# Fused attention and gated MLP on one core: weight loads moved in among the activations, and the start's hand-written order replaced

## The chip, the cores and the metric

The kernel runs on one core of a Trainium2 chip. Its engines work side by side, each through its own queue in order: TensorE (PE, matrix products), VectorE (DVE), ScalarE (ACT), GpSimd (POOL) and SyncE (SP), which here issues every DMA. The metric is the device time of one execution in microseconds (us); lower is better.

## The reference, cut to what matters

```python
def mab(q, kv):                      # attention without projections
    s = scale * (q @ kv.transpose(0, 2, 1))
    a = softmax(s)                   # over the last axis
    return a @ kv
h   = mab(I, x)                      # 32 inducing rows attend to 12416 rows of x, for each of 4 batches
y   = mab(x, h)                      # every row of x attends to the 32 rows of h
g   = y @ w_gate                     # 128 -> 1536
out = (g * sigmoid(g) * (y @ w_val)) @ w_out     # 1536 -> 128
```

x is float32. The three weight matrices arrive as float64, so they are 8 bytes an element in memory.

## The kernel before

**The main loop.** For each of four batches the rows of x are cut into 25 column blocks of 512 or 480 rows, and each block into 12 tiles (the 12 groups of 128 of the 1536 hidden units). A tile is a *front* (two PE products into PSUM, gate and value, from the block's attention weights `stack` and the projected weights `tw`), a *gate* (SiLU on ACT), a *value* (a product on DVE), a split of the result into a high and a low part (`h_hi`, mostly by ACT, and `h_lo`, mostly by POOL), and a *back* (three PE products with `wo_lo`, `wo_hi`, `wo_hi` into the output). The fronts run some tiles ahead of the backs. Steps of the next batch's attention are put in between.

**The start.** Everything up to the first tiles of batch 0 is a list of tokens, `START` and then `SECOND`, run one after the other; that order is the order of each engine's queue. For batch 0 x comes in seven chunks of 14 blocks of 128 rows (the last has 13). `lx` loads a chunk with features on the partitions, `ln` loads it with rows on the partitions; a chunk for which `ln` is left out is turned by PE transposes and copied out of PSUM (by ACT or DVE). `s1` scores a chunk and evacuates it on DVE, `ma`/`mb` find the maximum of a group of chunks, `e1` is the exponential on ACT, `eT` turns it in 32 by 32 blocks on DVE, `hq` accumulates h on PE. Chunks 0 to GA-1 form one group with its own maximum, the others a second. `ha`, `hb`, `hc`, `hd` put the groups together and give hT and hTs (h turned; the second one scaled). Steps `z0` to `z8` make the first block's attention weights by a short path of its own, and `pa`, `pk`, `pb`, `pm`, `pc` project one sixth of the gate and value weights with hT.

**The weights.** Nine pieces of 512 KB each (J0 to J5 of gate and value, o0 to o2 of the output) are loaded with `ld` and turned from float64 to float32 on the chip (class `Piece`): `X` and `low` on ACT, then `sh` and `jn` on DVE, then `add` on POOL. The output pieces are also split, `hi` on ACT and `lo` on POOL.

**Block 0** of batch 0 is an exception (`u.whole`): its backs use the joined float32 output weights as one product each, without a split of h, and the split output weights are made ready by the end of that block.

Of the kernel before, what the change touches and what calls it, by code (L numbers as in the profile page):

```python
# [76 lines left out]
jn:J3 pa:2 f:2 g:1 add:o0 m:0 pk:2 X:J4 sum:1 f:3 pm:2 add:J3 rec:1 m:1 g:2 X:o1 k:0 pa:3 pc:2 g:3 low:J4 sh:J4 m:2 f:4 f:5 jn:J4 k:1 pk:3 sh:o1 g:4
m:3 no:1:1 pm:3 k:2 at:1 X:J5 sh:J5 pc:3 g:5 low:J5 jn:J5 low:o1 jn:o1 add:J4 pa:4 add:J5 f:6 m:4 pk:4 m:5 g:6 pb:4 k:3 f:7 pa:5 m:6 add:o1 ah:1:1 f:8
al:1:0 g:7 X:o2 pk:5 sh:o2 g:8 low:o2 k:4 pm:5 f:9 jn:o2 pc:5 k:5 f:10 sp:1 m:7 k:6 m:8 f:11 g:9 add:o2 m:9 g:10 g:11 m:10 m:11 hi:o0 lo:o0 hi:o1
lo:o1  # L80
# [31 lines left out]
def induced_set_attention_then_swiglu(ctx: ExitStack, tc: tile.TileContext, xt, xn, ind, wgv, wo, out):  # L112
# [58 lines left out]
    class Piece:  # L171


        def __init__(self, work, k, i):
# [11 lines left out]
        def X(self):
            nc.scalar.activation(out=self.t.bitcast(F32), in_=self.hw.bitcast(F32), func=AF.Copy, scale=2.0 ** -112)

        def sh(self):
            nc.vector.tensor_scalar(out=self.t, in0=self.t, scalar1=3, scalar2=0x7FFFFFF8, op0=ALU.logical_shift_left, op1=ALU.bitwise_and)  # L190

        def jn(self):
            nc.vector.scalar_tensor_tensor(out=self.t, in0=self.hw, scalar=0x80000000, in1=self.t, op0=ALU.bitwise_and, op1=ALU.bitwise_or)
# [675 lines left out]
```

## Time and profile before

| what | value |
|---|---|
| device time, three executions | 1376.99, 1377.46, 1377.83 us |
| their median | 1377.46 us |
| profiled execution, first to last instruction (its span) | 1374.8 us |
| busy in the span: PE, ACT, DVE, POOL | 99%, 91%, 87%, 86% |
| granted clock of PE | 1.00 all through |

The profiled execution's own time is its span, 1374.8 us; the median of the timed executions is 2.7 us above it, and that difference is taken as the part outside the span. A time in a row counts from the start of the span. "Busy" is the share of time in which an engine has an instruction in flight; instructions of one engine overlap, so the distance from start to start says more about an engine's pace than the length of one row.

### The profile page before, as it was taken

How to read it: one execution, taken by the hardware profiler on the slowest of the kernel's cores; microseconds unless marked ns; L12 is line 12 of the kernel's file. 1: busy time of each engine (PE TensorE's matmuls, PEld its weight loads, DVE VectorE, ACT ScalarE, POOL GpSimd, SP SyncE). 2: the span in 40 equal slices, each digit the busy share in tenths (PEclk: the TensorE clock that was granted, in tenths of full speed). 3: DMA queues.
4: the chain of work that ended last, by engine and by line, in shares of the span. 5: the costliest groups of instructions: out<-in, count | busy, mean ns of one | idle time of the engine just before them, and what ended most of it. 6: DMA issues, size and time to landing. Idle time of an engine off the chain costs nothing.

```text
span 1374.8 us, 25215 instructions
## 1 busy us (share of the span) xinstructions
PE 1366.1 (99%) x7459; PEld 1183.8 (86%) x7459; DVE 1195.4 (87%) x2088; ACT 1245.7 (91%) x2380; POOL 1179.8 (86%) x994
## 2 busy tenths in 40 slices
...
GB/s 370 81 96 133 160 104 114 119 56 71 38 130 160 94 143 112 67 62 37 44 72 119 192 80 95 123 73 52 44 38 45 39 47 39 39 46 38 43 44 22
DMA packets 50680, 119.49 MB, mean 87 GB/s; under 512 B 11376, under 2 KB 28272, under 8 KB 50544
## 3 DMA queue, kind: packets, MB, share of 16 engines
...
## 4 chain that ended last, share of the span: by engine, by line
PE 97%; ACT 1%; DMA 1%; DVE 1%; issue 0%; SPq 0%; DVEq 0%
PE o L737 18%; PE gv L694 18%; PE gv L695 18%; PE o L738 18%; PE o L739 18%; PE gv L275 2%; PE o L323 1%; PE o L275 1%; DMA xt_sb<-xt 1%; PE o L734 0%; ACT silu L700 0%; PE gv L424 0%; PE gv L267 0%; ACT xn_sb L184 0%; DVE eT L313 0%
## 5 line engine op out<-in xcount | busy, mean ns | idle before, releaser
L718 POOL TENSOR_TENSOR h_lo<-h,h_hi 128x512 fp32r<-128x512 f32 (+1 forms) x889 | 1088.6, 1250 | 147.7 <-ACT h_hi L716 104.7
L700 ACT ACTIVATE silu<-gv 128x512 f32<-128x512 f32 (+1 forms) x1200 | 704.8, 589 | 95.5 <-PE gv L694 69.9
L708 DVE TENSOR_TENSOR h<-gv,silu 128x512 f32<-128x512 f32 (+1 forms) x891 | 590.9, 669 | 90.5 <-PE o L738 50.7
L716 ACT CAST h_hi<-h 128x512 fp32r<-128x512 f32 (+1 forms) x778 | 468.9, 603 | 0.8 <-DVE h L708 0.8
L694 PE MATMUL gv<-stack,tw 128*128 128x512 f32 (+1 forms) x1200 | 452.7, 377 | 1.3 <-DVE stack L544 1.0
L695 PE MATMUL gv<-stack,tw 128*128 128x512 f32 (+1 forms) x1200 | 448.2, 374 | 0.0
L737 PE MATMUL o<-h_hi,wo_lo 128*128 128x512 f32 (+1 forms) x1188 | 445.6, 375 | 0.0
L739 PE MATMUL o<-h_lo,wo_hi 128*128 128x512 f32 (+1 forms) x1188 | 443.2, 373 | 0.0
L738 PE MATMUL o<-h_hi,wo_hi 128*128 128x512 f32 (+1 forms) x1188 | 443.2, 373 | 0.0
L708 DVE TENSOR_TENSOR gv<-gv,silu 128x512 f32<-128x512 f32 (+1 forms) x297 | 201.5, 678 | 66.0 <-PE o L738 46.0
L694 PEld LDWEIGHTS gv<-stack,tw 128*128 128x128 f32 x1200 | 227.0, 189 | 33.9 <-ACT tw L416 3.0
L737 PEld LDWEIGHTS o<-h_hi,wo_lo 128*128 128x128 f32 x1188 | 224.8, 189 | 33.4 <-issue 10.6
L695 PEld LDWEIGHTS gv<-stack,tw 128*128 128x128 f32 x1200 | 227.0, 189 | 28.0 <-ACT silu L700 1.6
L739 PEld LDWEIGHTS o<-h_lo,wo_hi 128*128 128x128 f32 x1188 | 224.8, 189 | 24.3 <-POOL h_lo L718 0.3
L738 PEld LDWEIGHTS o<-h_hi,wo_hi 128*128 128x128 f32 x1188 | 224.8, 189 | 23.2
L718 DVE TENSOR_TENSOR h_lo<-gv,h_hi 128x512 fp32r<-128x512 f32 (+1 forms) x297 | 197.6, 665 | 0.8
L716 ACT CAST h_hi<-gv 128x512 fp32r<-128x512 f32 (+1 forms) x295 | 168.8, 572 | 10.1 <-DVE gv L708 8.4
L211 DVE TENSOR_REDUCE h_hi<-h 128x512 fp32r<-128x512 f32 (+1 forms) x113 | 73.7, 661 | 0.0
L748 DVE COPY ob<-o 128x512 f32<-128x512 f32 (+1 forms) x99 | 65.8, 665 | 0.2 <-PE o L739 0.2
L484 POOL TENSOR_TENSOR a_lo<-aT,a_hi 128x480 fp32r<-128x480 f32 (+2 forms) x26 | 29.9, 1151 | 0.0
L196 POOL TENSOR_TENSOR wgv_sb<-s_all 128x512 int32<-128x512 int32 x2 | 2.9, 1487 | 28.4 <-ACT s_all L184 28.4
L471 POOL TENSOR_TENSOR s_all<-s_all,sm 128x512 f32<-128x512 f32 (+2 forms) x27 | 26.1, 966 | 0.0
...
## 6 DMA issues: line engine op xcount, KB each, us to landing
...
```

Of the source, the lines that this page charges most:

```text
L211: nc.vector.tensor_reduce(out=out, in_=in_.unsqueeze(2), op=ALU.max, axis=AX.X)
L275: nc.tensor.matmul(out=ps[32 * j:32 * j + 32, 32 * (lo - b0):32 * (hi - b0)], lhsT=lhsT, rhs=st.xt[q][:, lo - CH0[q]:hi - CH0[q], j, :], s ...
L694: nc.tensor.matmul(out=u.g[:, :n], lhsT=st.w[:, wcol(0, t)], rhs=rhs, start=True, stop=True)
L695: nc.tensor.matmul(out=u.v[:, :n], lhsT=st.w[:, wcol(1, t)], rhs=rhs, start=True, stop=True)
L700: nc.scalar.activation(out=u.s[:, :u.n], in_=u.g[:, :u.n], func=AF.Silu)
L708: nc.vector.tensor_mul(out=u.h[:, :n], in0=u.v[:, :n], in1=u.s[:, :n])
L716: u.cast(out=u.hi[:, :n], in_=u.h[:, :n])
L718: eng.tensor_sub(out=u.lo[:, :n], in0=u.h[:, :n], in1=u.hi[:, :n].bitcast(F32))
L737: nc.tensor.matmul(out=o[:, :n], lhsT=wo_lo[:, ws], rhs=hi, start=(t == 0), stop=False)
L738: nc.tensor.matmul(out=o[:, :n], lhsT=wo_hi[:, ws], rhs=hi, start=False, stop=False)
L739: nc.tensor.matmul(out=o[:, :n], lhsT=wo_hi[:, ws], rhs=lo, start=False, stop=(t == NT - 1))
L748: (nc.scalar.copy if u.last else nc.vector.tensor_copy)(out=ob[:, :n], in_=o[:, :n])
```

## The change

It touches the start and the first block alone.

- **Loads.** One output piece is loaded between chunks 2 and 3 of x, and J4, o1 and J0 ahead of the only chunk that still comes by `ln` (chunk 5). Six chunks are turned on PE in place of four and a third. The chunks come in the order 0, 1, 4, 2, 3, 6, 5, and `GA` is 5: chunks 0 to 4 form the first group.
- **Buffers.** `Piece` converts in place: `X`, `sh` and `jn` of a J piece work in its final place in `wgv_sb`. The raw J pieces lie in two `tw` buffers; the projected weights later take the first of them over.
- **Finer tokens.** Steps that were one token are split into their PE part and the part of the other engine (`s1p`/`s1e`, `tp`/`te`, `mbp`/`mbe`, `hdp`/`hds`/`hdt`, `fg`/`fv`), and both lists of tokens are written anew.
- **Block 0** loses its exception: its h is split like any other (`c` on ACT, once on DVE, and `l` on POOL or DVE) and its backs are three products with the split output weights.
- **z0** scores four column groups with hTs as the stationary operand, and a DVE transpose (`z0t`) puts the result in order.

```diff
-GA = 4
+GA = 5
 START = """
-lx:0:0:4 lx:0:4:14 lx:1 lx:2 lx:3 lx:4 lx:5 lx:6 ln:4 ln:5 ln:6:0:8 ld:J0:s0 ld:J1:s1 ld:J2:t0 ld:J3:t1 wm:9
+lx:0:0:4 lx:0:4:14 lx:1 wm:9 tp:0:0 wm:6 te:0:0:1 lx:4 tp:0:3 tp:0:1 tp:0:2 te:0:1:1 s1p:0 te:0:2:0 te:0:3:1 lx:2 s1p:1 s1e:0 tp:1:0 s1e:1 tp:1:2 te:1:0:1 tp:1:3 te:1:2:0
...
 class Piece:
...
-            self.t = work[:, 2 * WP:3 * WP].bitcast(U32)
             self.w = work[:, 2 * WP:3 * WP] if k == "o" else wgv_sb[:, self.cs]
+            self.t = self.w.bitcast(U32)
...
         def z0():
             st.zps = psum()
-            for t in range(FC[0]):
-                nc.tensor.matmul(out=st.zps[:, M * t:M * t + M], lhsT=st.xt[0][:, t].rearrange("c j r -> c (j r)"), rhs=st.hTs, start=True, stop=True)
+            scores(st.hTs, 0, FC[0], st.zps)
+
+        def z0t():
+            st.z = sgl.tile([P, FC[0], M], F32, name="z")
+            nc.vector.transpose(out=st.z.rearrange("p t m -> p (t m)"), in_=st.zps[:, :M * FC[0]])
...
-        tw = att.tile([P, 2 * DFF], F32, name="tw")
-        bufs |= {f"t{i}": tw[:, 3 * WP * i:3 * WP * i + 3 * WP] for i in range(2)}
+        tws = [att.tile([P, 2 * DFF], F32, name="tw") for _ in range(2)]
+        bufs = {f"{k}{i}": t[:, 2 * WP * i:2 * WP * i + 2 * WP] for k, t in zip("tu", tws) for i in range(3)}
+        bufs |= {f"s{i}": s_all[:, 3 * WP * i:3 * WP * i + 3 * WP] for i in range(2)}
...
     def value(u):
         n = u.n
-        if u.whole:
-            u.h = hip.tile([P, WF], F32, name="h_hi")
-        else:
-            u.h = u.v if u.t in DVE_TILES else hp.tile([P, WF], F32, name="h")
+        u.h = u.v if u.t in DVE_TILES else hp.tile([P, WF], F32, name="h")
...
-        if u.whole:
-            k = t % (WP // P)
-            nc.tensor.matmul(out=o[:, :n], lhsT=pieces[f"o{t // (WP // P)}"].w[:, P * k:P * k + P], rhs=u.h[:, :n], start=(t == 0), stop=(t == NT - 1))
-        else:
-            hi, lo = turns(u.hi[:, :n]), turns(u.lo[:, :n])
-            nc.tensor.matmul(out=o[:, :n], lhsT=wo_lo[:, ws], rhs=hi, start=(t == 0), stop=False)
...
+        hi, lo = turns(u.hi[:, :n]), turns(u.lo[:, :n])
+        nc.tensor.matmul(out=o[:, :n], lhsT=wo_lo[:, ws], rhs=hi, start=(t == 0), stop=False)
+        nc.tensor.matmul(out=o[:, :n], lhsT=wo_hi[:, ws], rhs=hi, start=False, stop=False)
+        nc.tensor.matmul(out=o[:, :n], lhsT=wo_hi[:, ws], rhs=lo, start=False, stop=(t == NT - 1))
```

Three places show how the queues change. The first is the queue of SP (the loads) from the third x transfer on, before; `xn` rows are `ln` loads, `wgv` and `wo` are pieces J and o.

```order
L243 DMA xt_sb<-xt 128x1792 x3
L243 DMA xt_134<-xt 128x1792
L243 DMA xt_136<-xt 128x1792
L243 DMA xt_138<-xt 128x1664
L258 DMA xn_140<-xn 128x1792
L258 DMA xn_142<-xn 128x1792
L258 DMA xn_144<-xn 128x1024
L181 DMA s_all<-wgv 128x1024 x2
L181 DMA tw<-wgv 128x1024 x2
L181 DMA xn_sb<-wo 128x1024
L181 DMA xn_sb<-wgv 128x1024 x2
L181 DMA s_all<-wo 128x1024 x2
```

The same stretch of SP's queue after the change:

```order
L250 DMA xt_155<-xt 128x1792
L250 DMA xt_sb<-xt 128x1792
L181 DMA s_all<-wo 128x1024
L250 DMA xt_sb<-xt 128x1792
L250 DMA xt_248<-xt 128x1024
L250 DMA xt_248<-xt 128x640
L250 DMA xt_276<-xt 128x1792
L181 DMA tw<-wgv 128x1024
L181 DMA s_all<-wo 128x1024
L181 DMA tw<-wgv 128x1024
L265 DMA xn_363<-xn 128x1792
L181 DMA tw<-wgv 128x1024 x4
```

The first output piece (s_all<-wo) now stands ahead of chunk 3 of x, two J pieces and the second output piece stand ahead of the one `xn` load that is left, and four J pieces follow it.

The second place is DVE's queue around hTs, the first step behind h, before. L190 and L193 are `sh` and `jn` of a weight piece, L511 and L515 are `z1` and `z2`, L445 turns the scores of the second block.

```order
L390 TENSOR_SCALAR hTs<-gv 128x32
L190 TENSOR_SCALAR s_all<-s_all 128x512
L193 SCALAR_TENSOR_TENSOR s_all<-s_all 128x512
L190 TENSOR_SCALAR s_all<-s_all 128x512
L193 SCALAR_TENSOR_TENSOR s_all<-s_all 128x512
L511 TENSOR_REDUCE zm<-gv 128x4
L515 TENSOR_TENSOR z<-gv,zm 128x128
L445 STREAM_TRANSPOSE s_all<-gv 128x512
L207 TENSOR_REDUCE pairs<-z 128x4
```

After the change, from three rows ahead of hTs on (L196 and L199 are now `sh` and `jn`, L416 is `hc`, L551 is `z0t`, L555 and L558 are `z1` and `z2`):

```order
L199 SCALAR_TENSOR_TENSOR wgv_sb<-tw,wgv_sb 128x512
L416 SCALAR_TENSOR_TENSOR hn<-o,fac,hn 128x128
L196 TENSOR_SCALAR wgv_sb<-wgv_sb 128x512
L424 TENSOR_SCALAR hTs<-gv 128x32
L199 SCALAR_TENSOR_TENSOR wgv_sb<-tw,wgv_sb 128x512
L551 STREAM_TRANSPOSE z<-gv 128x128
L196 TENSOR_SCALAR wgv_sb<-wgv_sb 128x512
L555 TENSOR_REDUCE zm<-z 128x4
L196 TENSOR_SCALAR wgv_sb<-wgv_sb 128x512
L558 TENSOR_TENSOR z<-z,zm 128x128
L486 STREAM_TRANSPOSE s_all<-gv 128x512
L196 TENSOR_SCALAR wgv_sb<-wgv_sb 128x512
```

A `sh` now stands between `hc` and hTs, and a weight step before nearly every step of the z path.

The third place is PE's queue around the first back of block 0, before (L694 and L695 are a front, L402 and L413 `pa` and `pm`, L734 a back):

```order
L695 MATMUL gv<-stack,tw 128x512
L413 MATMUL gv<-tw,below 128x512
L734 MATMUL o<-h_hi,xn_sb 128x512
L402 MATMUL gv<-wgv_sb,hT 128x512
L694 MATMUL gv<-stack,tw 128x512
L695 MATMUL gv<-stack,tw 128x512
L694 MATMUL gv<-stack,tw 128x512
L695 MATMUL gv<-stack,tw 128x512
L734 MATMUL o<-h_hi,xn_sb 128x512
L413 MATMUL gv<-tw,below 128x512
L734 MATMUL o<-h_hi,xn_sb 128x512
```

After the change (L738 and L743 are the two halves of a front, L454 is `pm`, L787 to L789 a back):

```order
L738 MATMUL gv<-stack,tw 128x512
L454 MATMUL gv<-tw,below 128x512
L743 MATMUL gv<-stack,tw 128x512
L787 MATMUL o<-h_hi,wo_lo 128x512
L788 MATMUL o<-h_hi,wo_hi 128x512
L789 MATMUL o<-h_lo,wo_hi 128x512
L738 MATMUL gv<-stack,tw 128x512
L787 MATMUL o<-h_hi,wo_lo 128x512
L788 MATMUL o<-h_hi,wo_hi 128x512
L789 MATMUL o<-h_lo,wo_hi 128x512
L743 MATMUL gv<-stack,tw 128x512
L738 MATMUL gv<-stack,tw 128x512
```

The first back comes after five and a half fronts in place of four fronts, and it is three products instead of one. From the first back of block 1 on (12 backs and 19 fronts issued, in both kernels) the rows of PE are the same in both.

## Rows read from the trace of the kernel before

**Rows 1.** The page: its span, then busy time and share of each engine.

```profile
span 1374.8 us, 25215 instructions
...
PE 1366.1 (99%) x7459; PEld 1183.8 (86%) x7459; DVE 1195.4 (87%) x2088; ACT 1245.7 (91%) x2380; POOL 1179.8 (86%) x994
```

**Rows 2.** Busy time by stretch: PE, PEld, DVE, ACT, POOL; then PE clock, DMA share, GB/s.

```profile
12.80:19.00 6.20, 6.17 (x62) 3.68 (x66) 4.08 (x12) 3.86 (x9) 0.00 (x0) 1.00 1.03 422
38.00:50.00 12.00, 11.11 (x32) 5.12 (x30) 10.76 (x21) 11.85 (x23) 7.81 (x6) 1.00 0.00 1
...
62.06:1374.80 1312.74, 1309.18 (x6975) 1148.34 (x6973) 1150.37 (x1984) 1202.24 (x2296) 1159.02 (x967) 1.00 0.25 80
```

**Rows 3.** The chain that ended last: start, length, what; first 100 us.

```profile
3.08 9.60 DMA xt_sb<-xt
...
50.61 0.86 PE o L734 x2
```

**Rows 4.** Timeline of PE: start, length, line, tiles, count, and what idle time ended on.

```profile
36.80 0.48 PE L694 MATMUL gv<-stack,tw 128*128 128x512 f32 x1 [1.02 <-DVE stack L544]
...
62.06 0.38 PE L737 MATMUL o<-h_hi,wo_lo 128*128 128x512 f32 x1
...
63.14 0.38 PE L737 MATMUL o<-h_hi,wo_lo 128*128 128x512 f32 x1
```

**Rows 5.** Timeline of ACT, 15 to 40 us, same columns.

```profile
15.43 0.67 ACT L307 ACTIVATE s_all<-s_all,negmax 128x448 f32<-128x448 f32 x1
...
18.57 0.68 ACT L307 ACTIVATE s_all<-s_all,negmax 128x448 f32<-128x448 f32 x1
...
19.23 0.66 ACT L307 ACTIVATE s_all<-s_all,negmax 128x448 f32<-128x448 f32 x1
...
29.57 0.70 ACT L184 ACTIVATE s_all<-s_all 128x512 int32<-128x512 uint32 x1
30.16 0.70 ACT L187 ACTIVATE tw<-tw 128x512 f32<-128x512 f32 x1
...
36.69 1.28 ACT L548 ACT_TABLE_LOAD   x1
...
38.09 0.58 ACT L700 ACTIVATE silu<-gv 128x512 f32<-128x512 f32 x1
```

**Rows 6.** Timeline of DVE, 23 to 34 us.

```profile
23.60 1.65 DVE L313 STREAM_TRANSPOSE eT<-s_all 128x448 f32<-128x448 f32 x3
...
26.37 0.16 DVE L361 TENSOR_REDUCE r<-gv 128x1 f32<-128x2 f32 x1 [0.89 <-PE gv L359]
...
27.68 0.35 DVE L384 SCALAR_TENSOR_TENSOR hn<-o,fac,hn 128x128 f32<-128x128 f32 x1
...
28.72 0.42 DVE L190 TENSOR_SCALAR s_all<-s_all 128x512 uint32<-128x512 uint32 x1
29.17 0.69 DVE L193 SCALAR_TENSOR_TENSOR s_all<-s_all 128x512 uint32<-128x512 uint32 x1
29.78 0.42 DVE L190 TENSOR_SCALAR s_all<-s_all 128x512 uint32<-128x512 uint32 x1
...
30.84 0.28 DVE L511 TENSOR_REDUCE zm<-gv 128x4 f32<-128x128 f32 x1
...
33.42 0.41 DVE L190 TENSOR_SCALAR tw<-tw 128x512 uint32<-128x512 uint32 x1
33.76 0.68 DVE L457 TENSOR_TENSOR s_all<-s_all,mx2a 128x512 f32<-128x512 f32 x1
```

**Rows 7.** Timeline of POOL, 38 to 42 us.

```profile
38.31 1.52 POOL L196 TENSOR_TENSOR xn_sb<-xn_sb 128x512 int32<-128x512 int32 x1 [1.85 <-ACT sl L548]
39.79 1.29 POOL L196 TENSOR_TENSOR wgv_sb<-tw 128x512 int32<-128x512 int32 x1
41.05 1.26 POOL L471 TENSOR_TENSOR s_all<-s_all,sm 128x512 f32<-128x512 f32 x1
```

**Rows 8.** Timeline of DVE: the join that starts beside POOL's third row above.

```profile
42.07 0.79 DVE L193 SCALAR_TENSOR_TENSOR xn_sb<-xn_sb 128x512 uint32<-128x512 uint32 x1
```

More of the change, by code (lines that the diff above doesn't have):

```diff
@@ L77 @@
[L77 to L80, printed above, removed]
+sh:J1 hdp X:J3 wm:2 add:J0 hds low:J3 jn:J1 z0 sM:4:20 X:J2 z0t sh:J3 hdt lo:o0 z1 low:J2 sh:J2 pa:4 z2 X:J5 sT:4:20 pa:0 add:J1
@@ L81 @@
+fg:11 k:6 m:10 c:9:0 fv:11 g:11 l:8 l:9 m:11
 """
@@ L83 @@
     12: "sp:2",
-    13: "hi:o2",
-    14: "lo:o2",
     15: "sp:3",
@@ L186, in X, with low @@
[L186 to L193, printed above, removed]
+        def low(self, e=0):
+            if e:
+                nc.gpsimd.tensor_scalar(out=self.lw.bitcast(I32), in0=self.lw, scalar1=2.0 ** -29, scalar2=None, op0=ALU.mult)
+            else:
+                nc.scalar.activation(out=self.lw.bitcast(I32), in_=self.lw, func=AF.Copy, scale=2.0 ** -29)
@@ L366, in hacc2 @@
         def hacc2(q):
[L367 to L371 removed]
+            g = int(q >= GA)
+            n0 = (0, CH0[GA])[g]
+            if g not in st.h2:
+                st.h2[g] = ps_o.tile([P, 512], F32, name="o")
+                n = (CH0[GA], NTB - CH0[GA])[g]
+                for k in range(NG):
+                    st.hleft[g, k] = [(n - k + NG - 1) // NG, True]
             for i in range(CH[q]):
[L373 to L374 removed]
+                k = (CH0[q] + i - n0) % NG
+                left = st.hleft[g, k]
+                left[0] -= 1
                 nc.tensor.matmul(
[L376 to L377 removed]
+                    out=st.h2[g][32 * k:32 * k + 32, 0:C], lhsT=st.eT[q][:, 32 * i:32 * i + 32], rhs=st.xn[q][:, i, :],
+                    start=left[1], stop=left[0] == 0)
+                left[1] = False
         def h2_b():
@@ L666, in induced_set_attention_then_swiglu @@
             at=f["aT"], ah=lambda q, e=0: f["a_hi"](q, (same, nc.scalar.copy)[e]),
-            al=lambda q, e=1: f["a_lo"](q, dve_pool[e]), sp=f["spread"], **{f"z{i}": f[f"z{i}"] for i in range(9)})
+            al=lambda q, e=1: f["a_lo"](q, dve_pool[e]), sp=f["spread"], z0t=f["z0t"], **{f"z{i}": f[f"z{i}"] for i in range(9)})
         for token in START.split():
@@ L756, in first, with cast @@
     def first(t):
-        made.append(front(cur, 0, 0, t))
+        made.append(front_g(cur, 0, 0, t))
         pend.append(made[t])
-    short |= dict(f=first, g=lambda t: gate(made[t]), m=lambda t: value(made[t]), k=lambda t: back(pend.pop(0)))
+    def cast(t, e):
+        made[t].cast = (nc.scalar.copy, same)[e]
+        high(made[t])
+    short |= dict(fg=first, fv=lambda t: front_v(made[t]), g=lambda t: gate(made[t]), m=lambda t: value(made[t]),
+                  c=cast, l=lambda t: low(made[t]), k=lambda t: back(pend.pop(0)))
     for token in SECOND.split():
         run(token)
+    wait += [u for u in made if u.lo is None]
     cur.steps = [(slot, lambda token=token: run(token)) for slot, tokens in FIRST.items() for token in tokens.split()]
```

191 lines of the change are left out of this document (110 added, 81 removed).

## The prediction

> **What bounds the kernel now.** I read the page first: of a span of 1374.8 us PE is busy for 1366.1 [rows 1]. A busy PE need not be at its peak, so I split the span at one row. At 62.06 us PE starts the first back of block 1 [rows 4]; behind it PE is busy for 1309.2 of 1312.7 us at full clock, more than ACT, DVE and POOL [rows 2], and the change leaves the rows of every queue behind that point as they were, but for a few positions. So the part behind 62.06 us keeps its length, about 1312.7 us, and the whole effect of the change is how much earlier or later that one row starts. I call it the handover. The median of the timed runs is 2.66 us above the span; I add the shift to the median.
>
> Ahead of the handover three engines share the binding. Up to about 13 us the chain is the DMA: chunk 3 of x lands at 3.08 + 9.60 = 12.7 us [rows 3], and the loads run at 422 GB/s [rows 2]. The first exponential starts at 15.43 [rows 5], 2.75 us behind that landing. Then come h and the z path, through DVE, to the first front at 36.80, which waited for DVE's last step of `stack` [rows 4]. From 38 to 50 us ACT is busy for 11.85 of 12 us and PE for 11.11 [rows 2]: ACT leads.
>
> **The loads.** Before, four chunks of x (3.67 MB) land ahead of the first maximum. Now chunk 4 and piece o0 stand ahead of chunk 3 as well: 0.92 + 0.52 = 1.44 MB more, 3.4 us at 0.42 MB a us. Chunk 3 lands at 16.1, and with the same 2.75 us behind it the first exponential starts at 18.9. That is a loss of 3.4 us at the head. What it buys is that weight pieces come among the chunks, so o0, o1, J4 and J0 are converted while ACT would have been idle; the ACT row at 15.43 is one of seven exponentials that before were spread with gaps over 9 us.
>
> **DVE from 18.9 us to the first front.** DVE is the queue through which the path runs, and its new order puts 7 `sh` and 7 `jn` into this stretch, where the old order had three `jn` and four `sh` ahead of the first front. Start-to-start distances, from [rows 6]: three `eT` in 1.65, so 0.55 each; `sh` 0.45 when its `jn` follows (28.72 to 29.17) and 0.34 when something else follows (33.42 to 33.76), so 0.40; `jn` 0.61 (29.17 to 29.78); r, hn and its second half as one block from 26.37 to 28.03, 1.66; `z1` to `z5` with the transposed scores and their maximum as one block from 30.84 to 33.42, 2.58. The sum: seven `eT` 3.85; seven `sh` 2.8; seven `jn` 4.3; the two blocks 4.24; three copies of turned chunks and two score evacuations 2.2 (my estimate, the size of an `eT` or less); waiting for PE to score chunks 6 and 5, 0.7 (estimate); hTs, `z0t` and six one-column steps 1.6 (estimate); `pb` and the two last steps of `stack` 1.6 (estimate, at most a `jn` each). Together 21.3 us, so the first front starts at 40.2 in place of 36.80: **3.4 us later**.
>
> ACT in the same stretch is nearly as full: seven exponentials at 0.66 (18.57 to 19.23), 15 `X` and `low` at 0.59 (29.57 to 30.16), the table load and what goes with it 1.4 (36.69 to 38.09), all from [rows 5], and some 13 shorter steps of 0.1 to 0.5, 5.3 by estimate: 4.6 + 8.9 + 1.4 + 5.3 = 20.2, so its first SiLU could start at 39.1 to 39.6. It is not the later of the two, but it gives the lower end: if DVE's sum is too high, the first front cannot come before about 39.
>
> **PE from the first front to the handover.** Here the change saves. Before: 19 fronts at 0.43 us (two fifths of a tile, of which five products take 63.14 - 62.06 = 1.08 us [rows 4]) are 8.2; 12 float32 backs at 0.86 [rows 3] are 10.3; four `pa`, the same shape, 3.4; four `pm` 0.9; sum 22.8. The trace has 62.06 - 36.80 = 25.26, so PE waited 2.45. After: the fronts 8.2; 12 backs of three products, 36 x 0.216 = 7.8; three `pa` 2.6 (the fourth now stands ahead of the first front); one `pm` 0.2; sum 18.75, **4.05 less**. The price of the split backs is ten casts more on ACT and twelve `l`, nine of them on POOL at about 1.27 [rows 7]. Their cover is that nearly all of `X` and `low` is done by then. ACT in block 0 then has two operations a tile, at 0.5 each (an estimate: a SiLU lasts 0.58 [rows 5] and the next operation starts a little ahead of its end), 1.0 against PE's 1.08; without the cover it would bind.
>
> The waits in this stretch stay about the same, I take 2.5 us. The first back still stands behind the fourth and fifth front, which need PSUM buffers that `pk` and `pb` of late pieces hold, so PE waits 1.3 to 2 us there; and the stack of block 1 is sent by SP after `al`, in a block that now takes 17 us rather than 24, so its last transfer may keep the first front of block 1 for about 0.5.
>
> **The sum.** First front +3.4, products -4.05, waits +0.05: the handover moves from 62.06 to 61.45, -0.6 us, and the median from 1377.46 to **1376.9 us**. A measurement of this kernel tells about 0.2%, 2.75 us, from no change; this lies well within it.
>
> [...] One POOL `add` takes 1.52 us where its like takes 1.29 [rows 7], and a `jn` that starts at 42.07, when POOL's row at 41.05 runs until 42.31, takes 0.79 [rows 8] where one beside an idle POOL takes 0.69 [rows 6]. So the rows show some 0.1 to 0.25 us for a meeting. [...] Ten POOL operations now lie between 28 and 43 us beside as many `sh` and `jn`. [...] I take 0.5 of such cost as already inside the `jn` distances, and keep the rest as a rival.
>
> **Rivals.**
>
> (A) The helpers do not hold PE up: DVE's sum is 1 us too high (more pairs at 0.34, no waiting for chunk 5), and behind the first front PE waits only for the stack, 0.5. Then the handover is at 39.2 + 18.75 + 0.5 = 58.4, and the time 1373.8 us. For it: ACT's own sum allows 39.1, and casts are at 0.5. Against: ACT, DVE and POOL are all nearly full from 27 to 45 us, and any of them late makes the others wait. It counts as faster from a handover ahead of 59.3 on.
>
> (B) DVE and POOL block each other, at one place: between 28 and 43 us, in the joins. A `jn` or `sh` that comes while a POOL operation runs waits for its end, as the one at 42.07 may have: half of 1.29 on average, 0.64. At six meetings of ten on the path it is +3.8, the handover is at 65.3 and the time 1380.7. It counts as slower from 5.3 meetings on (3.35 / 0.64). For it: 1.52 and 0.79 above. [...]
>
> [...]
>
> **How the numbers follow.** Forecast with (C), within 0.2% of before: 0.56. (A), faster by over 0.2%: 0.25. (B), slower by over 0.2%: 0.19. The range reaches from (A)'s time, a little below, to (B)'s, a little short of it: 1373.6 to 1380.2. The forecast's own range is 1375.2 to 1378.6, from DVE's sum less 1 us with the same waits up to three meetings of 0.64.
>
> **What would show it.** Right: the first exponential near 18.9, the first front near 40, the handover within 60 to 63, and the same 1312 to 1313 us behind it. DVE nearly full from 19 to 40 us. Wrong: a first front ahead of 39 (then DVE's sum is the wrong step), one behind 42 with `jn` rows of 1 us and more (then B), a handover less than 20 or more than 23 us behind the first front (then the waits are), or a part behind the handover that differs by over 1 us, which would mean that the order of the start reaches further than I think.

## The result, and the profile after

The changed kernel takes 1386.35 us (median of five, 1385.73 to 1386.90) where the kernel before, run beside it, takes 1377.46: a ratio of 1.0064, 95% interval 1.0052 to 1.0076. It is **8.9 us slower**. The prediction was 1376.9 us, within 1373.6 to 1380.2, so it is wrong, and with it the case that it held likeliest (no change).

The page of the changed kernel, its span and its busy times, against [rows 1]:

```profile
span 1384.1 us, 25302 instructions
...
PE 1368.6 (99%) x7487; PEld 1188.8 (86%) x7487; DVE 1206.7 (87%) x2094; ACT 1253.8 (91%) x2396; POOL 1192.6 (86%) x1003
```

PE's work is hardly changed (1368.6 for 1366.1 us); the span grew by 9.3. As in the prediction I split the span at the handover, the first back of block 1. Busy time by stretch (PE, PEld, DVE, ACT, POOL, then PE's granted clock, DMA share, GB/s), against [rows 2]:

```profile
43.00:45.00 2.00, 0.00 (x0) 0.00 (x0) 1.94 (x5) 1.29 (x3) 2.00 (x2) 1.00 0.00 0
...
46.00:49.00 3.00, 3.00 (x7) 1.65 (x6) 2.89 (x5) 2.29 (x5) 1.51 (x2) 0.50 0.00 0
...
61.00:63.00 2.00, 0.00 (x0) 0.02 (x1) 1.94 (x4) 1.47 (x3) 1.27 (x1) 0.92 0.46 113
63.00:66.00 3.00, 2.99 (x7) 2.44 (x8) 1.61 (x3) 1.72 (x4) 1.01 (x1) 0.50 0.39 96
...
70.85:1384.10 1313.25, 1309.56 (x6975) 1147.07 (x6973) 1150.82 (x1984) 1202.60 (x2296) 1159.76 (x966) 1.00 0.25 80
```

The last row shows that the part behind the handover is what it was: 1313.25 us for 1312.74. So 8.8 of the 9.3 us lie ahead of it. The other rows show two stretches in which PE did nothing (43 to 45 and 61 to 63), and behind each some 3 us at a granted clock of 0.50; before, the clock stood at 1.00 there. PE's timeline gives the places (start, length, line, tiles, count, and what the idle time in brackets ended on), against [rows 4]:

```profile
45.03 0.48 PE L738 MATMUL gv<-stack,tw 128*128 128x512 f32 x1 [2.45 <-DVE stack L586]
...
63.01 0.76 PE L738 MATMUL gv<-stack,tw 128*128 128x512 f32 x1 [2.19 <-DMA stack<-a_lo]
...
63.99 0.63 PE L787 MATMUL o<-h_hi,wo_lo 128*128 128x512 f32 x1
...
70.85 0.38 PE L787 MATMUL o<-h_hi,wo_lo 128*128 128x512 f32 x1
```

The first front starts at 45.03 (36.80 before, 40.2 predicted) and waited for DVE's last step of `stack`. The first front of block 1 at 63.01 waited 2.19 us for a DMA, the stack of block 1. The row at 63.99 lasts 0.63 where the same product lasts 0.38 at the full clock. The handover is at 70.85 (62.06 before, 61.45 predicted).

Further ahead, the first exponential on ACT's timeline, and two lines of the chain that ended at 75 us (start, length, what): chunk 3's transfer, and that of the stack.

```profile
19.46 0.67 ACT L325 ACTIVATE s_all<-s_all,negmax 128x448 f32<-128x448 f32 x1
```

```profile
4.35 12.35 DMA xt_sb<-xt
...
60.90 1.97 DMA stack<-a_lo
```

Chunk 3 landed at 4.35 + 12.35 = 16.7 and the first exponential started at 19.46; the head is close to what was predicted (16.1 and 18.9). Against before, 4.0 of the 8.8 us are lost up to the first exponential (15.43 before), 4.2 from there to the first front (25.57 us for 21.37), and 0.6 from there to the handover (25.82 for 25.26). The first loss was forecast, as 3.4; in the other two stretches the forecast had 21.3 and 21.25. DVE's timeline says why its stretch took 25.57 (L392 is the last small step of h's scaling, L196 `sh`, L199 `jn`, L525 `al`):

```profile
29.32 1.15 DVE L392 TENSOR_SCALAR fac<-fac,r 128x2 f32<-128x2 f32 x1
...
30.98 1.51 DVE L199 SCALAR_TENSOR_TENSOR wgv_sb<-tw,wgv_sb 128x512 uint32<-128x512 uint32 x1
...
32.67 1.47 DVE L196 TENSOR_SCALAR wgv_sb<-wgv_sb 128x512 uint32<-128x512 uint32 x1
...
34.17 1.66 DVE L199 SCALAR_TENSOR_TENSOR wgv_sb<-tw,wgv_sb 128x512 uint32<-128x512 uint32 x1
...
36.48 1.31 DVE L196 TENSOR_SCALAR wgv_sb<-wgv_sb 128x512 uint32<-128x512 uint32 x1
...
40.22 2.16 DVE L199 SCALAR_TENSOR_TENSOR wgv_sb<-tw,wgv_sb 128x512 uint32<-128x512 uint32 x2
...
44.89 0.68 DVE L213 TENSOR_REDUCE pairs<-s_all 128x16 f32<-128x512 f32 x1
...
57.35 0.69 DVE L757 TENSOR_TENSOR h<-gv,silu 128x512 f32<-128x512 f32 x1
57.96 1.72 DVE L525 TENSOR_TENSOR a_lo<-aT,a_hi 128x512 fp32r<-128x512 f32 x1
```

And POOL's at the same times (L202 `add`, L208 `lo`, L498 `sb`, L767 `l`):

```profile
29.14 1.30 POOL L202 TENSOR_TENSOR wgv_sb<-wgv_sb,tw 128x512 int32<-128x512 int32 x1
30.56 1.38 POOL L208 TENSOR_TENSOR wo_lo<-s_all,wo_hi 128x512 fp32r<-128x512 f32 x1
...
32.56 1.29 POOL L202 TENSOR_TENSOR wgv_sb<-wgv_sb,tw 128x512 int32<-128x512 int32 x1 [0.56 <-DVE wgv_sb L199]
33.81 1.47 POOL L208 TENSOR_TENSOR wo_lo<-s_all,wo_hi 128x512 fp32r<-128x512 f32 x1
35.97 1.55 POOL L202 TENSOR_TENSOR wgv_sb<-wgv_sb,tw 128x512 int32<-128x512 int32 x1 [0.68 <-ACT wgv_sb L193]
...
41.91 4.55 POOL L202 TENSOR_TENSOR wgv_sb<-wgv_sb,tw 128x512 int32<-128x512 int32 x3 [0.68 <-ACT stack L583]
...
55.20 3.94 POOL L767 TENSOR_TENSOR h_lo<-h,h_hi 128x512 fp32r<-128x512 f32 x3 [0.96 <-ACT h_hi L761]
```

Read the two together. `sh` takes 0.42 and `jn` 0.69 beside an idle POOL [rows 6]; here they take 1.3 to 1.7. The step of L392 works on two columns and takes 1.15. Each of the first five long DVE rows ends behind the end of a POOL row, and by no more than its own length: 29.32 + 1.15 = 30.47 behind 29.14 + 1.30 = 30.44; 32.49 behind 31.94; 34.14 behind 33.85; 35.83 behind 35.28; 37.79 behind 37.52. The joins among them end 0.55 behind POOL's row, the `sh` 0.27 to 0.29. The six rows from 29.32 to 40.22 (the last of them two joins) last 9.26 us. Beside an idle POOL they would take 0.23 (as L364 in the kernel before, and in e1 below) + 2 x 0.69 + 2 x 0.42 + 1.29 (the pair of joins) = 3.74: **5.5 us more**. Not all DVE rows are held up. The reduction at 44.89 and the product of a value at 57.35 (one operand in PSUM) last 0.68 and 0.69 although POOL works beside them. Nor is the TENSOR_SCALAR of L390 on one column (0.15 us at 28.93, while a POOL row runs from 27.87 to 29.18).

### The profile page after: what moved, and what is told of

Its sections match the earlier page's. It is cut to its first block, busy times and chain, and to the rows that moved or that the text cites. A ratio compares the mean times of both kernels' runs of the same rounds, so it can differ in the third digit from the quotient of the medians.

```text
span 1384.1 us, 25302 instructions
## 1 busy us (share of the span) xinstructions
PE 1368.6 (99%) x7487; PEld 1188.8 (86%) x7487; DVE 1206.7 (87%) x2094; ACT 1253.8 (91%) x2396; POOL 1192.6 (86%) x1003
## 4 chain that ended last, share of the span: by engine, by line
PE 96%; DVE 1%; DMA 1%; ACT 1%; issue 1%; SPq 0%; DVEq 0%
PE o L787 18%; PE gv L738 18%; PE gv L743 18%; PE o L789 18%; PE o L788 18%; PE gv L282 2%; PE o L341 1%; DMA xt_sb<-xt 1%; PE o L282 1%; PE gv L465 0%; DVE wgv_sb L199 0%; PE gv L443 0%; ACT silu L752 0%; ACT h_hi L761 0%; DVE wgv_sb L196 0%
## 5 line engine op out<-in xcount | busy, mean ns | idle before, releaser
L767 POOL TENSOR_TENSOR h_lo<-h,h_hi 128x512 fp32r<-128x512 f32 (+1 forms) x898 | 1100.9, 1252 | 154.0 <-ACT h_hi L761 109.1
L761 ACT CAST h_hi<-h 128x512 fp32r<-128x512 f32 (+1 forms) x787 | 474.1, 603 | 1.1 <-DVE h L757 1.1
L738 PE MATMUL gv<-stack,tw 128*128 128x512 f32 (+1 forms) x1200 | 449.7, 375 | 4.8 <-DVE stack L586 2.4
L743 PE MATMUL gv<-stack,tw 128*128 128x512 f32 (+1 forms) x1200 | 450.3, 375 | 0.2 <-DVE h_lo L767 0.2
L787 PE MATMUL o<-h_hi,wo_lo 128*128 128x512 f32 (+1 forms) x1200 | 450.1, 375 | 0.0
L789 PE MATMUL o<-h_lo,wo_hi 128*128 128x512 f32 (+1 forms) x1200 | 447.8, 373 | 0.0
L738 PEld LDWEIGHTS gv<-stack,tw 128*128 128x128 f32 x1200 | 227.2, 189 | 34.9 <-DVE stack L586 3.3
L787 PEld LDWEIGHTS o<-h_hi,wo_lo 128*128 128x128 f32 x1200 | 227.1, 189 | 34.2 <-issue 10.7
L743 PEld LDWEIGHTS gv<-stack,tw 128*128 128x128 f32 x1200 | 227.3, 189 | 28.1 <-ACT silu L752 1.7
L789 PEld LDWEIGHTS o<-h_lo,wo_hi 128*128 128x128 f32 x1200 | 226.9, 189 | 25.3 <-POOL h_lo L767 0.6
L767 DVE TENSOR_TENSOR h_lo<-gv,h_hi 128x512 fp32r<-128x512 f32 (+1 forms) x300 | 199.7, 666 | 0.8
L525 POOL TENSOR_TENSOR a_lo<-aT,a_hi 128x480 fp32r<-128x480 f32 (+2 forms) x26 | 30.1, 1157 | 0.0
L202 POOL TENSOR_TENSOR s_all<-s_all 128x512 int32<-128x512 int32 x2 | 2.6, 1310 | 24.7 <-ACT xn L276 17.7
```

Source lines behind the costliest of these rows:

```text
L738: nc.tensor.matmul(out=u.g[:, :n], lhsT=st.w[:, wcol(0, t)], rhs=u.rhs, start=True, stop=True)
L743: nc.tensor.matmul(out=u.v[:, :u.n], lhsT=u.st.w[:, wcol(1, u.t)], rhs=u.rhs, start=True, stop=True)
L761: u.cast(out=u.hi[:, :u.n], in_=u.h[:, :u.n])
L767: eng.tensor_sub(out=u.lo[:, :n], in0=u.h[:, :n], in1=u.hi[:, :n].bitcast(F32))
L787: nc.tensor.matmul(out=o[:, :n], lhsT=wo_lo[:, ws], rhs=hi, start=(t == 0), stop=False)
L789: nc.tensor.matmul(out=o[:, :n], lhsT=wo_hi[:, ws], rhs=lo, start=False, stop=(t == NT - 1))
```

## Experiments

Theory 1, from these rows: DVE and POOL block each other in some of their instructions, and that makes the first front late. Theory 2: the weight pieces land late. Theory 3: what costs is the stretch behind the first front, its low clock and its wait for the stack. The kernel before was run again beside each group of kernels (1376.99 to 1377.58), so a difference between kernels of two groups is good to some 0.6 us.

**e1_no_adds: POOL cleared ahead of the first front.**

```diff
         def add(self):
-            nc.gpsimd.tensor_add(out=self.w.bitcast(I32), in0=self.t.bitcast(I32), in1=self.lw.bitcast(I32))
+            pass
...
-... jn:J0 lo:o1 wm:5 low:J1 hc
+... jn:J0 wm:5 low:J1 hc
...
-... hdt lo:o0 z1 ...
+... hdt z1 ...
...
-... fv:1 m:0 fg:2 pk:2 no:1:1 fv:2 m:1
+... fv:1 lo:o0 m:0 fg:2 pk:2 no:1:1 fv:2 m:1 lo:o1
```

> The changed kernel with POOL's additions of all nine weight pieces left out (the weights keep only the value of their high words) and POOL's two subtractions lo:o0 and lo:o1 moved behind the first front, so that POOL has one row of about 1 us before the first front. Theory 1, DVE and POOL block each other: the sh and jn rows go back to about 0.42 and 0.69, the small row of fac to about 0.24, the first front comes at 40 to 41 in place of 45.03, the handover near 66, the time 1380.5 to 1382.5. Theory 2, late loads of weights: those rows stay short in any case but wait for transfers, the first front stays near 45 and the time near 1386. Theory 3, it is the stretch behind the first front (a low granted clock and the wait for the stack) that costs, not DVE: the first front moves but the handover doesn't, 1385 to 1386.

Measured: 1381.54 us, ratio 1.0028 (1.0019 to 1.0038) to before, so 4.8 us come back. The same four steps on DVE's timeline as above, and two joins that still meet POOL (a `sb` at 36.52, a `lo` at 38.01); then PE's:

```profile
29.18 0.23 DVE L392 TENSOR_SCALAR fac<-fac,r 128x2 f32<-128x2 f32 x1
...
29.91 0.68 DVE L199 SCALAR_TENSOR_TENSOR wgv_sb<-tw,wgv_sb 128x512 uint32<-128x512 uint32 x1
...
31.47 0.42 DVE L196 TENSOR_SCALAR wgv_sb<-wgv_sb 128x512 uint32<-128x512 uint32 x1
...
32.24 0.68 DVE L199 SCALAR_TENSOR_TENSOR wgv_sb<-tw,wgv_sb 128x512 uint32<-128x512 uint32 x1
...
36.45 2.14 DVE L199 SCALAR_TENSOR_TENSOR wgv_sb<-tw,wgv_sb 128x512 uint32<-128x512 uint32 x2
```

```profile
41.23 0.48 PE L738 MATMUL gv<-stack,tw 128*128 128x512 f32 x1 [2.41 <-DVE stack L586]
...
58.84 0.45 PE L738 MATMUL gv<-stack,tw 128*128 128x512 f32 x1 [2.19 <-DMA stack<-a_lo]
...
65.17 0.38 PE L787 MATMUL o<-h_hi,wo_lo 128*128 128x512 f32 x1
```

Same rows, same order, and the short lengths are back; the first front is at 41.23, 3.8 us earlier, the handover at 65.17. Theory 1 is what the run bears out (the first front a little behind the 40 to 41 expected), and Theory 2 falls: the loads are the same, and no DVE row waits for one of the weight pieces. Without the additions the pieces are also ready earlier for PE's `pa`, so that this run by itself does not tell the two effects apart; e6 and e7 below do. Of the prediction's sum for DVE, 21.3 us from the first exponential (here 18.77) to the first front, 22.46 are measured, of which the two joins in the row of 2.14 us lose 0.85. The 2.19 us for the stack stay.

**e6_port: the meeting measured by itself.** Ahead of the kernel before, on scratch data:

```diff
+    for _ in range(3):
+        t_red()
+        t_jn()
+        t_sh()
+    t_red()
+    for i in range(8):
+        t_add(3 if i == 0 else 4)
+    for _ in range(4):
+        t_sh()
+        t_jn()
+    for _ in range(4):
+        t_jn()
```

> The kernel before with a measurement ahead of everything else, on a scratch part of wgv_sb: DVE does three times a reduction, a jn and a sh while POOL is idle; then POOL does eight additions while DVE does four pairs of sh and jn and four more jn. Its time as a kernel says nothing. If the two engines block each other, jn (0.69 alone) and sh (0.42 alone) beside POOL's additions last 1 to 2 us each and end where a POOL row ends, and POOL's rows are longer than 1.27 by about the part that DVE ran. If rows cost 0.1 to 0.25 a meeting, as the prediction took it, jn lasts 0.7 to 0.95 and sh 0.45 to 0.7 there. The sh has one SBUF input: if only instructions with two are held up, sh keeps 0.42.

From its one execution, DVE's timeline (L176 reduction, L170 `jn`, L173 `sh`; POOL idle from 4.73 to 11.14), and POOL's eight additions:

```profile
6.70 0.68 DVE L170 SCALAR_TENSOR_TENSOR wgv_sb<-wgv_sb 128x512 uint32<-128x512 uint32 x1
7.30 0.42 DVE L173 TENSOR_SCALAR wgv_sb<-wgv_sb 128x512 uint32<-128x512 uint32 x1
7.64 0.69 DVE L170 SCALAR_TENSOR_TENSOR wgv_sb<-wgv_sb 128x512 uint32<-128x512 uint32 x1
...
12.99 1.48 DVE L173 TENSOR_SCALAR wgv_sb<-wgv_sb 128x512 uint32<-128x512 uint32 x1
14.39 1.75 DVE L170 SCALAR_TENSOR_TENSOR wgv_sb<-wgv_sb 128x512 uint32<-128x512 uint32 x1
16.06 1.48 DVE L173 TENSOR_SCALAR wgv_sb<-wgv_sb 128x512 uint32<-128x512 uint32 x1
```

```profile
11.14 12.25 POOL L179 TENSOR_TENSOR wgv_sb<-wgv_sb 128x512 int32<-128x512 int32 x8 [6.41 <-DVE wgv_sb L176]
```

Alone, `jn` to `sh` is 0.60 and `sh` to the next step 0.34 (6.70, 7.30, 7.64). Beside POOL `sh` to `jn` is 1.40 and `jn` to `sh` 1.67: **1.06 us more for each**. POOL's additions go from 1.26 (39.79 to 41.05 in [rows 7]) to 12.25 / 8 = 1.53, 0.27 more. The pair's 3.07 is two of POOL's 1.53: one DVE step gets in for each POOL instruction, and POOL hardly slows, so DVE pays. The prediction's 0.1 to 0.25 us was too little by a factor of four or more. `sh`, with one SBUF input, is held up like `jn`: 1.48 us here for 0.42 alone. The reduction at 44.89 above, with POOL at work beside it, was not: 0.68, as long as the reductions of this run with POOL idle (at 6.11, 8.24 and 10.37).

**e2_z_first: the z path ahead of the joins.**

```diff
-... hq:6 sh:J0 hi:o1 ld:o2:x0 hb X:J1 jn:J0 lo:o1 wm:5 low:J1 hc
+... hq:6 hb hi:o1 ld:o2:x0 X:J1 wm:5 low:J1 sh:J0 hc
...
-z3 sh:J5 pk:4 z4 low:J5 pm:4 m2:4:20 wm:6 X:o2 z5 sb:4:20:1 jn:J2 ...
+z3 pk:4 z4 low:J5 z5 pm:4 m2:4:20 wm:6 X:o2 sb:4:20:1 sh:J1 pk:0 z6:1 pc:4 jn:J1 ...
```

> The changed kernel with nothing left out, but in DVE's queue the steps of the z path stand ahead of most sh and jn, and lo:o0, lo:o1 come later on POOL. Theory 1 (DVE's queue, lengthened by POOL, sets the first front): the first front comes at 40 to 42; what was saved is given back in part, since the fronts of pieces J2, J3 and J5 now wait for their joins; handover 68 to 71, time 1383.5 to 1386.5. Theory 2 (late loads): first front near 45, time 1386 or more.

Measured: 1388.43 us, 1.0081 (1.0066 to 1.0096). By its number this is Theory 2's, but ACT's timeline shows another wait:

```profile
40.00 0.59 ACT L446 CAST tw<-gv 128x512 fp32r<-128x512 f32 x1 [4.95 <-POOL wgv_sb L202]
```

ACT's first `pk` writes into the tile `tw`, in which pieces J4, J0 and J1 were loaded, so it waits until POOL's `add` of J1 (38.69 to 39.97), moved back in the order, has read its words, and PE idles for 4.81 us behind it. The run says nothing for or against the blocking. It does show that with these buffers the joins of the three pieces in `tw` cannot simply be moved back: the first `pk` waits for them.

**e3_early_stack: block 1's stack sent earlier.**

```diff
-... pk:5 fg:4 m:3 add:o2 c:2:0 fv:4 fg:5 pb:3 pm:5 g:4
+... pk:5 fg:4 m:3 at:1 add:o2 c:2:0 ah:1:1 fv:4 fg:5 pb:3 al:1:0 sp:1 pm:5 g:4
...
-fg:8 k:3 c:6:0 m:7 g:8 l:6 fv:8 fg:9 al:1:0 hi:o2 k:4 m:8 c:7:0 sp:1 fv:9 ...
+fg:8 k:3 c:6:0 m:7 g:8 l:6 fv:8 fg:9 hi:o2 k:4 m:8 c:7:0 fv:9 ...
```

> The changed kernel with the steps that make and send the stack of block 1 (at, ah, al, sp) some 5 us earlier in the order. Theory 3 (the wait of 2.2 us for that stack at 60.6 to 63.0, and the stretch at half clock behind it, are a cost of their own): the first front of block 1 waits for less than 0.5, the granted clock stays at 1.00 from 49 us on, the handover comes at 67 to 68 and the time is 1382.5 to 1383.5. Rival (the helpers are that late in any case, or al ahead of the gates delays the tiles of block 0 by as much): the idle time moves to another place before 63, the handover stays at 70 to 71 and the time at 1385.5 to 1387.

Measured: 1383.76 us, 1.0045 (1.0028 to 1.0061), 2.6 us less than the changed kernel. The gain is a little smaller than expected (handover 68.59 for 67 to 68, time above 1383.5). The first front is at 45.68; PE's timeline has the first front of block 1 and the handover:

```profile
62.33 0.38 PE L738 MATMUL gv<-stack,tw 128*128 128x512 f32 x1
...
68.59 0.38 PE L787 MATMUL o<-h_hi,wo_lo 128*128 128x512 f32 x1
```

The wait is gone (62.33, no bracket), the clock is 1.00 from 45 us on, and from the first front to the handover it takes 22.91 in place of 25.82. The 2.9 us are less than the 2.19 of the wait and the 1.6 of the slow rows together, since some short waits for ACT, DVE and POOL took their place. So Theory 3 is right for a part of the loss, beside Theory 1.

**e4_whole_block0: the split of block 0's backs undone.**

```diff
+        if u.whole:
+            k = t % (WP // P)
+            nc.tensor.matmul(out=o[:, :n], lhsT=pieces[f"o{t // (WP // P)}"].w[:, P * k:P * k + P], rhs=u.h[:, :n], start=(t == 0), stop=(t == NT - 1))
+        else:
+            hi, lo = turns(u.hi[:, :n]), turns(u.lo[:, :n])
+            nc.tensor.matmul(out=o[:, :n], lhsT=wo_lo[:, ws], rhs=hi, start=(t == 0), stop=False)
...
```

> The changed kernel with one part of the change undone: the twelve backs of block 0 are one float32 product each again, and their casts on ACT and subtractions l are left out. If PE's work sets the stretch, as the prediction had it, the handover comes 12 x (0.86 - 0.65) = 2.5 us later, at 73.4, and the time is 1388.9. If the helpers and waits set it, the split buys nothing here: handover at 70 to 71 or, with ACT and POOL relieved and the stack's steps earlier, at 68 to 70; time 1384 to 1386.5.

Measured: 1383.58 us, 1.0044 (1.0029 to 1.0059). It is 2.8 us *faster* than the changed kernel, with the longer products. The first front is at 44.71; on PE's timeline the first front of block 1 and the handover:

```profile
61.01 0.38 PE L738 MATMUL gv<-stack,tw 128*128 128x512 f32 x1
...
68.32 0.38 PE L802 MATMUL o<-h_hi,wo_lo 128*128 128x512 f32 x1
```

From first front to handover 23.61 us, with 2.5 us more of PE's work than in the changed kernel. The first front of block 1 doesn't wait (61.01, no bracket): `al` runs at its 0.68 us because POOL has no `l` to do, and the transfers pass beside the longer products. This is the same wait that e3 took away, reached from the other side. The split saves PE 2.5 us and costs more than that. How much of the cost is the wait with the slow clock behind it, and how much the work that the split adds on ACT, DVE and POOL, this run does not part.

**e5_warm: PE kept busy ahead of the first front.**

```diff
-sl z8:1 add:J3 z8:0 sum:1 fg:0 ...
+sl z8:1 add:J3 z8:0 wo:22 sum:1 fg:0 ...
```

> The changed kernel with 22 transposes of the identity, whose result nobody uses, put into PE's queue just ahead of the first front, where PE sits idle for 2.45 us. If the low granted clock at 45 to 49 us follows that idle time and costs by itself, the clock stays at 1.00 there, the rows at 45 to 49 last 0.38 in place of 0.63, the handover comes 1.0 to 1.7 us earlier and the time is 1384.7 to 1385.4. If ACT and DVE set that stretch, the rows are short again but PE waits as long in between: 1386 to 1386.6. The stretch at half clock at 63 to 66 us has its own idle time ahead of it and stays in either case.

Measured: 1386.70 us, 1.0062 (1.0047 to 1.0077), no gain. PE's timeline:

```profile
42.42 2.57 PE L693 MATMUL o<-ident 128*128 128x128 f32 x22
...
47.73 0.48 PE L743 MATMUL gv<-stack,tw 128*128 128x512 f32 x1 [0.69 <-DVE tw L450]
...
71.08 0.38 PE L792 MATMUL o<-h_hi,wo_lo 128*128 128x512 f32 x1
```

The transposes fill the idle time, and the clock stands at 1.00 from 40 to 63 us. PE then waits for DVE instead (0.69 at 47.73), and the handover is at 71.08. From the first front to the first back it takes 8.19 us (45.05 to 53.24) at full clock, 8.17 in the changed kernel, with some 3 us of it at half clock: the first slow stretch costs nothing, because the helpers set the pace there. Behind the wait for the stack the clock falls again (0.70 from 63 to 66 us).

**e7_adds_later: fewer POOL rows ahead of the first front, nothing left out.** On top of e4:

```diff
-X:J0 ha0 add:o1 eT:5 ... add:J4 hi:o0 hq:6 sh:J0 hi:o1 ld:o2:x0 hb X:J1 jn:J0 lo:o1 ...
+X:J0 ha0 eT:5 ... add:J4 hq:6 sh:J0 ld:o2:x0 hb X:J1 jn:J0 ...
...
-... m:3 add:o2 c:2:0 ...
+... m:3 add:o2 add:o1 c:2:0 ...
-g:5 m:4 fv:5 l:2 k:0 pc:5 m:5 c:3:0 fg:6 ... l:4 g:7
+g:5 m:4 fv:5 l:2 k:0 pc:5 m:5 c:3:0 hi:o0 lo:o0 fg:6 ... l:4 hi:o1 lo:o1 g:7
```

> The changed kernel with whole float32 backs in block 0 (as e4_whole_block0), which leaves the split weights of o0 and o1 unused until block 1, and so with POOL's addition of o1 and its two subtractions lo:o0, lo:o1, and ACT's hi:o0 and hi:o1, moved behind the first front. Nothing is left out. Three POOL rows fewer lie beside DVE ahead of the first front, which by the rows of e4_whole_block0 held up fac by 0.9, and two jn by 0.8 and 0.95. Theory 1: first front 2 to 2.7 us earlier than there (44.7), at 42 to 42.7; handover at 66 to 66.5; time 1381 to 1381.8. Rival: the other collisions take the place of those removed, first front 44 or later, time 1383 or more.

Measured: 1381.06 us, 1.0026 (1.0016 to 1.0035), as Theory 1 had it. The first front is at 42.92 and the handover at 66.08 on PE's timeline: 1.8 and 2.2 us earlier than in e4, and the time 2.5 us. DVE's timeline has two joins that in e4 take 1.51 and 1.66 us (at 30.65 and 33.85):

```profile
30.58 0.68 DVE L199 SCALAR_TENSOR_TENSOR wgv_sb<-tw,wgv_sb 128x512 uint32<-128x512 uint32 x1
...
33.00 0.69 DVE L199 SCALAR_TENSOR_TENSOR wgv_sb<-tw,wgv_sb 128x512 uint32<-128x512 uint32 x1
```

They are 1.80 us shorter together, which is the whole shift of the first front. The step of L392 was expected to be freed too and is not (1.00 us at 29.13): J4's addition now stands beside it. So POOL instructions moved aside are worth that much on DVE's queue with every addition still done.

**e8_late_load: the head's loss alone.** The kernel before with one useless load:

```diff
-lx:0:0:4 lx:0:4:14 lx:1 lx:2 lx:3 ...
+lx:0:0:4 lx:0:4:14 lx:1 lx:2 dl lx:3 ...
...
+            dl=lambda: nc.sync.dma_start(out=wgv_sb[:, :2816].bitcast(U32), in_=wgv[:, :2816]),
```

> The kernel before with one useless load of 1.44 MB (into wgv_sb, overwritten later) put ahead of chunk 3, as much as the change puts there, and nothing else. If the 3.4 us at the head go straight through to the first front and the handover, as the prediction had it, first exponential 18.9, first front 40.2, handover 65.5, time 1380.6. If part of it is absorbed by waits further on, less: 1378 to 1379.5.

Measured: 1381.45 us (1380.46 to 1382.94), 1.0028 (1.0018 to 1.0037): 3.9 us. The profiled execution is one of the longest (1382.74). PE's timeline (the scores of chunk 3, the handover) and the stretch around the first:

```profile
16.34 1.72 PE L275 MATMUL gv<-xt_sb,indT 128*32 128x448 f32 x8 [3.63 <-DMA xt_sb<-xt]
...
68.17 0.38 PE L738 MATMUL o<-h_hi,wo_lo 128*128 128x512 f32 x1
```

```profile
12.00:19.00 7.00, 3.37 (x21) 1.66 (x18) 1.44 (x5) 0.59 (x1) 0.00 (x0) 0.76 1.00 412
```

PE scores chunk 3 at 16.34, 3.5 us later than before, about the predicted 3.4. The first exponential moved by 5.05 (20.48), the first front by 6.07 (42.87) and the handover by 6.11, so in this execution nothing is absorbed. The excess over 3.5 came with the clock, granted at 0.76 in this stretch after PE had idled for 3.63 us, so that the eight scores at 16.34 last 1.72 in place of 0.96. Of the ten executions only the fastest has a mean clock of 1.000; it takes 1380.46, 2.9 us above before, so without the slow clock up to 0.6 us of the 3.5 may be absorbed. In the changed kernel PE turns chunk 4 in that time, and the clock stays at 1.00 from 12 to 19 us.

**e9_o_late and e10_x_first: two versions by hand, on top of e7.** e9 loads and converts o0 and o1 late; e10 also puts x first again.

```diff
-ld:o0:s0 tp:1:1 ... X:o0 ... sh:o0 low:o0 ... jn:o0 ... ld:o1:s1 ... X:o1 ... sh:o1 ... low:o1 ... jn:o1
+... ld:J5:u2 ld:o0:s0 ld:o1:s1 ... fv:1 m:0 low:o0 sh:o0 fg:2 ... jn:o0 add:o0 ... low:o1 sh:o1 ... jn:o1 add:o1
...
-GA = 5
+GA = 4
```

> e7_adds_later with the pieces o0 and o1 also loaded behind the weight pieces and converted behind the first front, where the whole backs need them. Nothing is left out. Chunk 3 lands 0.52 / 0.42 = 1.2 us earlier, and DVE has two sh and two jn less (2.0), POOL one addition less, ahead of the first front: if head and DVE add up as the rows say, first front 39.5 to 40.5 in place of 42.92, handover 63.5 to 65 (the four steps return behind the first front), time 1378.5 to 1380. If the other collisions or ACT take their place, the first front stays behind 41.5 and the time at 1380 to 1381.

> e9_o_late with x first as before: the first maximum over four chunks, chunk 4 loaded and scored behind chunk 3, still six chunks turned and the joins in place. Nothing is left out. The first exponential goes back to 15.4 to 16, 2 us or more ahead of e9_o_late; if that goes through to the handover, it comes at 61.5 to 63 and the time is 1376.5 to 1378.5, that of the kernel before or a little less. If the pieces of weights now come too late for the fronts, PE waits for them behind the first front and the time is 1379 or more.

Measured: 1381.84 us, 1.0031 (1.0020 to 1.0043), and 1384.05 us, 1.0049 (1.0034 to 1.0063). Both miss. In e9 the first exponential comes only 0.4 us earlier than in e7 (18.52 for 18.94, 1.2 expected) and the first front 1.55 us earlier (41.37), but the handover 1.2 us later (67.27): the clock is down behind the first front (0.77 from 40 to 45 us, where e7 has 1.00), the moved conversions now stand among the products of block 0 on DVE, and PE's timeline has waits for those products of 0.75 (at 49.11) and 0.98 us (at 59.88). In e10 the first exponential comes at 17.51, not at 15.4 to 16, and the first front at 44.82; I wrote that order by hand and it holds the second group of chunks up (its first exponential at 27.11, 24.76 in e7). It says nothing on the loads. No version tried here beats the kernel before.

**e11_both: e1 and e3 together.**

```diff
         def add(self):
-            nc.gpsimd.tensor_add(out=self.w.bitcast(I32), in0=self.t.bitcast(I32), in1=self.lw.bitcast(I32))
+            pass
...
-... m:3 add:o2 c:2:0 fv:4 fg:5 pb:3 pm:5 g:4
+... m:3 at:1 add:o2 c:2:0 ah:1:1 fv:4 fg:5 pb:3 al:1:0 sp:1 pm:5 g:4
```

> e1_no_adds and e3_early_stack together: POOL's additions of the nine pieces are left out (the weights keep only the value of their high words), lo:o0 and lo:o1 come behind the first front, and the stack of block 1 is made and sent some 5 us earlier. If these two are what the prediction's sum lacked, the rest of it holds: first front near 41.2 as in e1_no_adds, from there to the handover 23.94 less the 2.2 of the wait, 21.3 to 21.8 (the prediction had 21.25), handover at 62.5 to 63, time 1378 to 1379.5. If something else holds PE up, the wait moves to another place and the time stays at 1380 or more.

Measured: 1379.42 us (1378.60 to 1380.26), 1.0014 (1.0004 to 1.0024). PE's timeline:

```profile
41.29 0.79 PE L738 MATMUL gv<-stack,tw 128*128 128x512 f32 x1 [2.40 <-DVE stack L586]
...
64.71 0.38 PE L787 MATMUL o<-h_hi,wo_lo 128*128 128x512 f32 x1
```

The two cures nearly add up: 4.8 and 2.6 us apart, 6.9 together. First front 41.29 as expected, no wait at the first front of block 1; the handover at 64.71 is 1.7 us later than expected, and in this execution a slow stretch lies behind the first front (a clock of 0.66 from 40 to 45 us; the front at 41.29 lasts 0.79, not 0.48). 2.4 us above before remain.

## Why the prediction was wrong, step by step

- **Behind the handover, unchanged.** Right: 1313.25 for 1312.74.
- **The loads, +3.4 at the head.** Right: the first exponential at 19.46, not 18.9 (chunk 3 landed 0.6 later), but in the profiled executions of e1, e2, e4, e5, e7 and e11, which start alike, it stands at 18.77 to 19.22, in that of e3 at 20.29, so the 0.6 is at least in part scatter. e8 shows that such a loss goes through, all of it or nearly.
- **DVE's 21.3 us.** This is the first step that failed, in one term. Without meetings the sum comes out: 22.46 in e1, 21.6 less what its row of two joins loses. That it comes out so closely is partly luck: DVE's waits of 0.2 us and more in that stretch of e1 are 1.92 us, nearly all for PE, where the prediction had 0.7, so its estimates for other terms were too high by as much. What failed is "I take 0.5 of such cost as already inside the `jn` distances", with the price of a meeting at "0.1 to 0.25". The six rows shown lost 0.92 each, and e6 has 1.06. Since DVE then waits less for PE (one such wait of 0.57 is left), 4.3 of the 5.5 us reach the first front: 25.57.
- **PE's work, 18.75, 4.05 less.** Not measured by itself, but the rows of the backs at the full clock have the lengths assumed. e4 shows that the part of it that the split saves (2.5) bought nothing.
- **"The waits in this stretch stay about the same, I take 2.5 us."** The second step that failed. They are 25.82 - 18.75 = 7.1. Between the first front and the first back PE stands for 2.8, not "1.3 to 2" (8.17 us for 5.4 of products: six fronts, three `pa`, one `pm`). The stack, which "may keep the first front of block 1 for about 0.5", cost 2.19: `al` was itself held up by POOL's `l` (57.96, 1.72 us, 1.04 more than alone), and SP sent the transfer that the front waited for at 60.90. The slow rows behind it cost 63.01 to 66.10 for seven products that take 7 x 0.216 at full clock, 1.6 more; the prediction had no term for the clock. In e1, at full clock, the same stretch takes 6.33 us (58.84 to 65.17) for 7.84 here. e3 gets 2.9 of the 7.1 back.
- **The sum.** 61.45 + 0.6 (head) + 4.3 (DVE) + 4.6 (waits) = 70.9, for 70.85 measured. The three are differences of the same rows, so that they must add up; they say how the miss is shared out.
- **The rivals.** (B) was the mechanism, in its place and with its number of meetings (six rows; the prediction gave no reason for six of ten, so that is luck); its price, 0.64, took a DVE step to come at random into one POOL instruction. In e6, with one POOL instruction right behind the other, a step waits for nearly the whole of one (1.06 us, where POOL's takes 1.26 alone); why it is 0.92 in the changed kernel, where POOL has gaps of 0.1 to 0.7 us, was not worked out. Both signs that the prediction named for these failures came: a first front behind 42 with `jn` rows over 1 us, and a handover over 23 us behind the first front. (B) also had no part behind the first front, so that its 1380.7 falls short by 5.6. (A) is out: no helper kept up. (C), a late landing of J2 or J5, shows in no row: from 19 to 46 us none of the waits listed for PE, ACT and DVE in the changed kernel ended on a transfer.
- **The price of a meeting.** The row of 0.79 in [rows 8] seemed to allow two readings, a join slowed by 0.1 us, or one that waited until POOL's row at 41.05 was done. The second was the better, and e6 agrees (1.06 us for a step): the row ends at 42.86, 0.55 behind POOL's 42.31, as the held-up joins of the changed kernel do; it was a blocked join that came 0.24 us before the end of POOL's instruction, and I took the one cheap meeting of the trace for the price of all of them.

What stays open: why the clock fell in some executions and not in others (see the last section), and how much of the 2.4 us left in e11 is the head and how much the clock.
